# One chunk's rows turned by VectorE and DRAM loads instead of TensorE, the last tile's halves in PSUM banks of their own, its stores on two queues, and the order table written anew

## The chip, the cores and the metric

The kernel runs on one core of a Trainium2 chip. The metric is device time in microseconds of one launch, the median of several runs. Beside it stands one profiled execution, whose trace gives every row that is quoted here.

## What is computed

One transformer-like block over S = 2048 rows of D = 512 numbers, all in fp32, cut here to what matters:

```python
mod = (silu(c) @ w_mod)                       # six rows of 512: sa, ca, ga, sb, cb, gb
h = layernorm(x) * (1 + ca) + sa
q, k, v = split(h @ wqkv)                     # 32 heads of 16
phi(t) = concat(softmax(t @ w_phi), softmax(-(t @ w_phi)))
o = phi(q) (phi(k)^T v) / (phi(q) sum(phi(k)) + 1e-6)
x = x + ga * (o @ wo)
h = layernorm(x) * (1 + cb) + sb
x1 = h + shift(gelu(layernorm(h) @ w1)) @ w2  # quarters of the columns shifted by +1, -1, +2, -2 rows
x = x + gb * (x1 + gelu(layernorm(x1) @ w3) @ w4)
```

## The kernel before, in words

Rows are handled in 16 tiles of 128 and in 8 chunks of 256. Every exact product is made of three matmuls in a reduced format: each operand is split into a high and a low part (`hi_lo`, L480), and `three` (L471) issues high by high, high by low and low by high.

The work has three stages. The first goes over the chunks and forms k, v and q features and the running sums `kva` and `zacc` (groups named k, v, q, kv in the code). The second, `phase_a` (L950), goes over the chunks again: it finishes the attention (`num`), multiplies by `wo` (group o), normalises twice, and must then have the normalised rows turned, features on partitions, because the product with `w1` contracts over features. The third takes pairs of chunks through `w3` (`up`) and `w4` (`down_steps`) in products of seven instead of eight blocks, and `finish_rows` adds the residuals and stores the output.

In `phase_a` the turning is done by `to_T` (L902): four transposes of 128x128 on TensorE for each tile of 128 rows into a PSUM tile `pt`, then a high part by ScalarE or VectorE and a low part by VectorE. Elsewhere the kernel has another way: `normed` (L1152) writes rows whose columns are mixed in blocks of 32, lets VectorE turn the 32x32 blocks (`turn`, L686, tile `yt`), stores the tile to DRAM (`store_rows`), and loads it back with blocks exchanged by four DMAs (`load_turned`, L694). `turned_block` (L706) and `split_turned` (L716) are the same for a chunk; the list `BIAS["nturn"]` (L227) says which chunks of `phase_a` use them, and it is empty. Nothing else in the code decides it.

At the end of the third stage `down_steps` holds four PSUM tiles `ac` for a chunk. `acc[2]` and `acc[3]` belong to its two tiles of 128 rows, and each holds both halves of 256 columns in one bank. The remainder of F (96 rows of `w4`) is added by three matmuls of 512 columns per tile. In the very last chunk `finish_rows` adds and stores the halves one after the other; in the plan every PSUM tile counts as one piece, so the first half is not read before the last matmul into the other half is done. All stores and nearly all loads are issued from SyncE, whose queue works in order.

The order of all instructions is not found by the code but is written out: `ORDER` (L40) is a list of the numbers of some 2800 steps, with a letter where a step goes to another engine than its first choice (A, V, G), and `emit` runs through it. `SLOT` (L162) names the buffer of each tile. Each engine works through its own steps in this order, and waits where a step's operand is not there. In the trace a helper's line stands for its operations: L468 matmul, L477 transpose, L398 ScalarE, L415 VectorE, L417 GpSimd, L452 store.

Of the kernel before, what the change touches and what calls it, by code (L numbers as in the profile page):

```python
# [15 lines left out]
P = 128  # L16
# [144 lines left out]
)  # L161
SLOT = {  # L162
    "pp": "2112103775712644371760105367611260725752737061505556300230174572340654633645407076250504027663340302"
          "145552521507",
    "bd": "13",
    "w": "174625cd387165ad28cb09",
    "rk2": "5846",
    "x2": "9",
    "st": "1377h22bbb1155hh02hg88gbf79d90221",
    "mv": "0bh0e42j01f3f380d28hebh03dg0bc0bb",  # L170
# [193 lines left out]
def body(ctx: ExitStack, tc, x, wqk_t, wv_d, wo_d, w1_d, w2_d, w3_d, w4_d, c_d, wmod_d, id_d, cst_d, cst2_d, out):  # L364
# [7 lines left out]
    def T(tag, shape=(P, D), dt=FP):  # L372
        return plan.tile(shape, dt, tag)
# [1048 lines left out]
```

## Time and profile before

| | us |
|---|---|
| median of 3 runs (550.7 to 551.48) | 550.83 |
| the profiled execution's own time | 551.07 |
| its span, first to last instruction | 549.2 |
| TensorE busy | 541.0 |
| VectorE busy | 492.2 |
| GpSimd busy | 372.7 |
| ScalarE busy | 339.8 |

The profile's times are counted from the start of the span. Between the span and the profiled execution's own time lie 1.9 us, and that execution was 0.24 us above the median. A row of the timeline gives start, length, engine, line, operation, tiles and count, and in square brackets the idle time before it and what ended it.

### The profile page before, as it was taken

The page shows a single profiled execution, that of the slowest core. Times are in us where ns is not written, and L with a number is a line of the kernel's source. Part 1 is how long each engine was busy: PE and PEld are TensorE (multiplying, and loading weights), DVE is VectorE, ACT ScalarE, POOL GpSimd, SP SyncE. Part 2 cuts the span into 40 slices and gives each one's busy share as a digit, 9 for nine tenths or more (in the row PEclk, how much of TensorE's full clock was granted, in tenths as well). Part 3 has the DMA queues.
Part 4 walks back from the last instruction along what each step waited for, and adds up shares of the span by engine and source line. Part 5 has one row for each costly group of instructions (what it writes and reads, how often), then busy time and mean ns, then how long its engine had stood idle before and what let it go on. Part 6 is the DMA issues. An engine that isn't in the chain of part 4 may idle for free.

```text
span 549.2 us, 12264 instructions
## 1 busy us (share of the span) xinstructions
PE 541.0 (98%) x4474; PEld 484.0 (88%) x4474; DVE 492.2 (90%) x899; ACT 339.8 (62%) x800; POOL 372.7 (68%) x383
## 2 busy tenths in 40 slices
PE   7999999999999999999999999999999999999997
PEld 6888788888677887888889999999999999999996
DVE  4999999999999999999998988988889768988887
ACT  2799988734436896959898576873533535234430
POOL 2388988979599999998995264433655653355354
PEclk9999999999999999999999999999999999999999
DMA  8975364247485669886898899989469746592032
GB/s 320 350 242 211 109 186 157 77 140 235 135 225 183 194 205 296 253 271 233 234 309 315 274 351 328 361 329 326 192 184 389 245 174 237 191 356 87 1 117 76
DMA packets 63668, 124.89 MB, mean 227 GB/s; under 512 B 7060, under 2 KB 26772, under 8 KB 59512
## 3 DMA queue, kind: packets, MB, share of 16 engines
q1 hardware_dynamic: 63320, 124.04, 66.4%
q8 instruction: 35, 0.57, 0.5%
q14 instruction: 25, 0.20, 0.1%
q10 hardware_dynamic: 288, 0.07, 0.1%
HBM read 89.74 MB, written 34.35 MB: 226 GB/s over the span
## 4 chain that ended last, share of the span: by engine, by line
PE 84%; DVE 9%; DMA 2%; issue 2%; POOL 2%; ACT 1%; DVEq 0%; POOLq 0%
PE pp L468 32%; PE pa L468 28%; PE ac L468 20%; PE pt L477 3%; DVE q L439 2%; DMA mod<-in_wmod 1%; DVE k L439 1%; DVE pz L439 1%; DVE pT L688 1%; DVE ke L415 1%; DMA const<-in_c 1%; DVE qe L415 1%; POOL qe L417 1%; PE kva L468 1%; ACT n L398 0%
## 5 line engine op out<-in xcount | busy, mean ns | idle before, releaser
L468 PE MATMUL pp<-w,hh 128*128 128x512 f32 x576 | 138.2, 397 | 0.0
L468 PEld LDWEIGHTS pp<-w,hh 128*128 128x128 f32 x576 | 106.8, 188 | 25.3 <-issue 1.0
L468 PE MATMUL pa<-bH,wq 128*128 128x256 f32 x840 | 105.9, 281 | 0.0
L468 PE MATMUL ac<-w,gg 128*128 128x256 f32 x840 | 105.4, 281 | 0.0
L468 PEld LDWEIGHTS ac<-w,gg 128*128 128x128 f32 x840 | 102.9, 188 | 1.2
L468 PEld LDWEIGHTS pa<-bH,wq 128*128 128x128 f32 x840 | 102.7, 188 | 0.6
L417 POOL TENSOR_TENSOR gg<-cu,gg 128x128 fp32r<-128x128 f32 (+1 forms) x32 | 21.4, 675 | 40.7 <-PE ac L468 13.8
L468 PE MATMUL pp<-w,sh 128*128 128x512 f32 x192 | 47.9, 397 | 0.0
L468 PE MATMUL pp<-w,oT 128*128 128x512 f32 x192 | 47.1, 395 | 0.0
L468 PE MATMUL pa<-nT,w 128*128 128x256 f32 x384 | 46.2, 279 | 0.0
L468 PEld LDWEIGHTS pa<-nT,w 128*128 128x128 f32 x384 | 45.1, 188 | 0.9 <-ACT mv L592 0.2
L468 PEld LDWEIGHTS pp<-w,sh 128*128 128x128 f32 x192 | 35.1, 188 | 8.6 <-POOL sh L1050 0.5
L468 PEld LDWEIGHTS pp<-w,oT 128*128 128x128 f32 x192 | 35.6, 188 | 8.0
L585 POOL TENSOR_TENSOR rs<-mv,const 128x2 f32<-128x2 f32 x31 | 24.3, 785 | 24.5 <-ACT mv L592 22.9
L398 ACT ACTIVATE cu<-pa 128x512 f32<-128x512 f32 (+1 forms) x41 | 21.3, 525 | 31.0 <-PE pa L468 13.6
L398 ACT ACTIVATE gg<-cu 128x256 fp32r<-128x256 f32 (+1 forms) x48 | 16.5, 360 | 25.0 <-PE ac L468 22.4
L417 POOL TENSOR_TENSOR e<-e,q 128x1024 f32<-128x1024 f32 x15 | 29.9, 2009 | 0.0
L415 DVE TENSOR_TENSOR gg<-sg,gg 128x512 fp32r<-128x512 f32 x36 | 26.3, 736 | 4.0 <-ACT gg L398 2.7
L417 POOL TENSOR_TENSOR ez<-e,const 128x1024 f32<-128x1024 f32 x12 | 28.8, 2407 | 0.1
L417 POOL TENSOR_TENSOR ke<-ke,k 128x1024 f32<-128x1024 f32 x14 | 28.6, 2049 | 0.0
L398 ACT ACTIVATE gg<-sg 128x512 fp32r<-128x512 f32 x28 | 17.3, 625 | 18.1 <-DVE gg L407 6.7
L415 DVE TENSOR_TENSOR cu<-pa,cu 128x512 f32<-128x512 f32 (+1 forms) x36 | 21.0, 594 | 7.5 <-PE pa L468 5.9
(221 smaller groups left out, 1224.7 us busy)
## 6 DMA issues: line engine op xcount, KB each, us to landing
wq<-dram SPq DMA_DIRECT2D x32, 1024.0 KB, 7.3
dram<-ws SPq DMA_DIRECT2D x35, 256.0 KB, 3.9
dram<-qe SPq DMA_DIRECT2D x16, 512.0 KB, 3.5
e<-dram SPq DMA_DIRECT2D x64, 128.0 KB, 3.6
xl<-in_x SPq DMA_DIRECT2D x30, 256.0 KB, 3.9
raw<-in_w SPq DMA_DIRECT2D x18, 256.0 KB, 4.0
mod<-in_wmod SPq DMA_DIRECT2D x16, 256.0 KB, 4.9
dram<-xl SPq DMA_DIRECT2D x16, 256.0 KB, 3.8
```

The costliest lines, as they stand in the source:

```text
L398: nc.scalar.activation(o(), i(), func, **kw)
L415: dve = ("DVE", 71 + 1.04 * o.n + 90 * (isps(a) and isps(b)), lambda: nc.vector.tensor_tensor(o(), a(), b(), op=op))
L417: pool = ("Pool", cost, lambda: nc.gpsimd.tensor_tensor(o(), a(), b(), op=op))
L439: plan.op("DVE", 65 + 1.04 * a.n + 110 * isps(o), lambda: nc.vector.tensor_reduce(o(), a(), axis=AX.X, op=op), [o], [a])
L468: nc.tensor.matmul(o(), a(), b(), start=s, stop=e, **kw)
L477: nc.tensor.transpose(o(), i(), ident())
L585: plan.op("Pool", 540 + 10 * m, lambda: nc.gpsimd.tensor_tensor(r(), v(), mhalf[:, :m](), op=OP.pow), [r], [v, mhalf])
L688: plan.op("DVE", 71 + 1.04 * o.n, lambda: nc.vector.transpose(o(), i()), [o], [i])
```

## The change

It has four parts.

1. `BIAS["nturn"]` is `[7]`: the last chunk's rows in `phase_a` take the way over VectorE and DRAM. Eight transposes on TensorE go, with the two high and two low parts that read `pt`. Two turns on VectorE, two stores, four loads and two high and two low parts that read SBUF come.
2. In the last chunk the second tile's halves stand in PSUM banks of their own (`apart_` and `acc[3]`). The remainder's three matmuls of 512 columns for that tile become six of 256, and the second half is complete once its three are done.
3. The store of that tile's first half, which is now the last to be ready, is issued from ScalarE's queue; the second half's store stays on SyncE's.
4. `ORDER` and `SLOT` are written anew over the whole kernel. Beside the places below, some steps change engine: in the first stage some 15 steps leave VectorE and 13 come to it; in the third stage the steps that cut the activations to pieces move both ways.

```diff
-    "0 3 16 1 6 2 30 23 44 4 48 46 5 50 8 89 13 82 7 14 20 9 143 37 671 38 39 31 40 24 78G 41 142 32 15 33 12 27 25 "
+    "0 3 23 6 2 16 30 44 5 46 48 50 8 1 15 12G 27 9 14G 81 13G 10 7 11 80G 43G 24 31 79 4 32 37 89 82 38 39 33 143 "
...
-        6, 8, 9, 10, 11, 12, 13, 14, 15], "tw": "any", "zpe": [15], "nturn": [], "xturn": []}
+        6, 8, 9, 10, 11, 12, 13, 14, 15], "tw": "any", "zpe": [15], "nturn": [7], "xturn": []}
...
         acc = [T("ac", [P, 2, HD]) for _ in range(4)]
+        apart_ = T("ac", [P, HD]) if c == NC - 1 else None
...
                     sl = slice(t * P, (t + 1) * P)
+                    if t and apart_ is not None:
+                        for o, n, whole in ((apart_, slice(HD, D), True), (acc[3][:, 0, :], slice(HD), False)):
+                            mms(three(o, g[:n9, 0, sl], g[:n9, 1, sl], last["w4"][0][:n9, n], last["w4"][1][:n9, n], whole, whole),
+                                [o], [g, *last["w4"]], skip=True)
+                        continue
...
-                finish_rows(c, acc)
+                finish_rows(c, acc, apart_)
...
             for a in range(2):
-                tt(x1[:, a, :], x1[:, a, :], p[:, a, :], OP.add)
-                store(out[rows_, a * HD:(a + 1) * HD], x1[:, a, :], P * HD * 4)
+                tt(x1[:, a, :], x1[:, a, :], apart_ if t and a else p[:, a, :], OP.add)
+                if t and not a:
+                    plan.op("Activation", 60, lambda dst=out[rows_, :HD], i=x1[:, 0, :]: nc.scalar.dma_start(dst, i()), [], [x1[:, 0, :]],
+                            land=2400)
+                else:
+                    store(out[rows_, a * HD:(a + 1) * HD], x1[:, a, :], P * HD * 4)
```

The loop over `a` runs over 0 and 1; the new table puts the add of `apart_` ahead of the other.

The new table at three places. The first is TensorE's start. `mod` are the pieces of `w_mod`, `pt` the first chunk's turned rows. Before, one transpose group stands ahead of the last piece of `w_mod`:

```order
L468 MATMUL pp_183<-mod_11_91,const_180 32x256 x4
L477 MATMUL pt_202<-const_71,xn_188 128x128
L477 MATMUL pt_202<-const_71,xn_174 128x128
L477 MATMUL pt_202<-const_71,xn_188 128x128
L477 MATMUL pt_202<-const_71,xn_174 128x128
L468 MATMUL pp_183<-mod_14_100,const_180 32x256 x4
L477 MATMUL pt_214<-const_71,xn_188 128x128
```

Now, on the same engine:

```order
L469 MATMUL pp_180<-mod_11_91,const_118 32x256 x4
L469 MATMUL pp_180<-mod_12_93,const_118 32x256 x4
L478 MATMUL pt_207<-const_97,xn_178 128x128
L478 MATMUL pt_207<-const_97,xn_191 128x128
L478 MATMUL pt_207<-const_97,xn_178 128x128
L478 MATMUL pt_207<-const_97,xn_191 128x128
L478 MATMUL pp_214<-const_97,mod_212 128x128 x2
L478 MATMUL pt_217<-const_97,xn_178 128x128
```

All four pieces of `w_mod` now come first, and both transpose groups behind them; the set of steps ahead of the first projection is the same.

The second place is SyncE's queue where the last chunk of `phase_a` is turned. `h` are the rows that `w2` leaves, `raw` pieces of `w4`, `yt` turned rows, `zt` and `bL` the tiles loaded back. Before:

```order
L452 DMA dram_4170<-h_3282 128x512
L691 DMA dram_4176<-yt_4167 128x512
L445 DMA raw_4183<-in_w 128x512
L691 DMA dram_4176<-yt_4200 128x512
L452 DMA dram_4233<-h_3652 128x512
L445 DMA raw_4248<-in_w 128x512
L445 DMA xl_4251<-dram_4170 128x512
```

Now the chunk's own two stores (to dram_4179) and its four loads stand in that queue:

```order
L692 DMA dram_4179<-yt_4169 128x512
L692 DMA dram_4179<-yt_4173 128x512
L453 DMA dram_4192<-h_3291 128x512
L446 DMA raw_4195<-in_w 128x512
L446 DMA raw_4200<-in_w 128x512
L453 DMA dram_4218<-h_3633 128x512
L699 DMA zt_4237<-dram_4179 32x8x128 x4
L446 DMA xl_4263<-dram_4192 128x512
```

Two stores of `h` and two loads of `raw` stand between the stores of `yt` and the loads of `zt`, and the loads of the next pair of chunks (`xl`) behind them.

The third place is the end of TensorE's program. `ac_7447` is the last tile's accumulator, `gl` the remainder's activations. Before:

```order
L468 MATMUL ac_7447<-w_4598,gg_7320 128x256 x2
L468 MATMUL ac_7447<-w_4598,gg_7420 128x256
L468 MATMUL ac_7447<-w_1947,gl_7353 128x512 x3
L468 MATMUL ac_7447<-w_4650,gg_7363 128x256
L468 MATMUL ac_7447<-w_4695,gg_7363 128x256
L468 MATMUL ac_7447<-w_4650,gg_7437 128x256
```

Now `ac_7537` is the bank apart and `ac_7428` the other half's:

```order
L469 MATMUL ac_7537<-w_1986,gl_7366 128x256 x3
L469 MATMUL ac_7428<-w_4628,gg_7335 128x256 x2
L469 MATMUL ac_7428<-w_4628,gg_7364 128x256
L469 MATMUL ac_7428<-w_1986,gl_7366 128x256 x3
L469 MATMUL ac_7428<-w_4636,gg_7356 128x256
L469 MATMUL ac_7428<-w_4757,gg_7356 128x256
L469 MATMUL ac_7428<-w_4636,gg_7417 128x256
```

The second half is complete nine matmuls of 256 columns ahead of the end.

More of the change, by code (lines that the diff above doesn't have):

```diff
@@ L40 @@
 ORDER = (
[120 rows of a table removed]
[120 rows of a table added]
 )
 SLOT = {
-    "pp": "2112103775712644371760105367611260725752737061505556300230174572340654633645407076250504027663340302"
-          "145552521507",
-    "bd": "13",
+    "pp": "2017153341420272046716375311663140363222230515024276010257257623475043673604407762257504025763345262"
+          "267543421715",
+    "bd": "0i",
     "w": "174625cd387165ad28cb09",
[L167 to L170, printed above, removed]
@@ L171 @@
-    "rs": "29812hcbbjji851d0ie93863874jh6213",
-    "nm": "3fa4a54dde4e1jjcf2883583gaacj278gb331h60ed7ha0092e635b5a",
-    "xn": "10cg751eba368fe9",
-    "mod": "lh9g7ejf9i4638bkia",
-    "mod2": "0213",
+    "rk2": "1090",
+    "x2": "4",
+    "st": "200009ff736hb70d77884j2978da427f0",
+    "mv": "56672ff476h030h70ff4j26b9idb3hhaj",
+    "rs": "04b499hc30b4740d748hi7d90hb225200",
+    "nm": "31g3i74fg434h7c4h30b0aaa722dchicd26ab6gff226975d725fjff7",
+    "xn": "e0kg751e4i36b430",
+    "mod": "4a9g740f9i4638bkbi",
@@ L176 @@
+    "mod2": "2356",
     "kva": "4",
     "za": "7",
-    "hh": "30a89be0",
-    "pt": "06254521753213317025344576360400",
-    "raw": "da1k0d63f6hg40cljd4940abi353",
-    "k1": "2430035525435132",
+    "hh": "3da89be0",
+    "pt": "365135427532573005233464601705",
+    "raw": "daj1gd7l15dc780fjd4940abi353",
+    "k1": "1051002221432452",
     "ke": "4501639451823940",
-    "k2": "1213035252034134",
-    "vv": "ib4j953cdj19a75f",
-    "qe": "3792232883214942",
-    "q1": "2440243225135053",
-    "qt": "5e97g70fkccg",
@@ L188 @@
-    "xl": "abd42002jf51cl836e2i1h3b0j5g2je53k0hhej4hlahd0",
-    "acc": "cl8hi",
-    "kvs": "f",
-    "pz": "1",
-    "q2": "10141003",
-    "e": "5617956758034928",
-    "ez": "8348813999970750",
-    "q3": "2212223043334222",
-    "q5": "23253203",
-    "pT": "4272394975373487",
-    "oT": "99594b24",
-    "nT": "9999bb2e",
-    "n": "1931gfgfahafb63g",
+    "k2": "1215311215032431",
+    "vv": "98lf042l7k4k95i1",
+    "qe": "0792222881213942",
+    "q1": "3035311003431055",
+    "qt": "5e0ii8c5dc36",
@@ L201 @@
+    "xl": "l8d32h02jf518j041lb2gh3b01fg2je53k5hhej4hlafd0",
+    "acc": "cl8h6",
+    "kvs": "c",
+    "pz": "1",
+    "q2": "32131223",
+    "e": "5617946758034928",
+    "ez": "8338271399150770",
+    "q3": "0010002203000422",
+    "q5": "33200011",
+    "pT": "6852384627273007",
+    "oT": "9b44ee04",
+    "nT": "b9bb4b2e",
+    "n": "8b40f00iahajb63g",
     "h": "7kd9l62c7i1lfkcd",
-    "gf": "17555662",
-    "sh": "2520ecb0",
-    "pa": "762553462761040036271541705740316243253470661263027034160772",
+    "gf": "17537312",
@@ L205 @@
+    "sh": "e902ecb0",
+    "pa": "565753556037500036267547305740315243253470661263027054360772",
     "wr": "80061",
-    "ws": "khe217da8lk4eba05bb5dfgfd71i652ak90",
+    "ws": "khe21adb1ei66jai5e29gfjfd71e652ak9g",
+    "zt": "1",
+    "yt": "47e59k0dj7j90lb6aa",
     "gb": "8",
-    "tw": "98935",
+    "tw": "96935",
     "bL": "47604149",
-    "nb": "1ahb5c79egg4jc3f",
-    "yt": "e5jkbdh7j9l9a6cd",
-    "bH": "52804219431594595069127578657523",
-    "tr": "714eb039akdl4172",
+    "nb": "bfhbca79egg4jc3f",
@@ L214 @@
+    "bH": "52804210431994595069127578657523",
+    "tr": "21ga5j3e6hdlg17b",
     "wq": "490c934e174e3174e7314e7134ee3417e431",
-    "cu": "672egi14f3fl25b7c10g4hg9ked6l14g9cd0jblf",
-    "gl": "c3jca56i",
-    "ac": "26311567160267423016415376013542",
-    "gg": "32781952372584716531287609873295063284107962583012103241806937415809263740821596",
-    "sg": "bkbka76k6hk6h4kj6a25j37b2lbji26k2i2594k2",
+    "cu": "672egi14b3fl25b7c10g4hg9ked6l14g9cd0jblf",
+    "gl": "c3jca56f",
+    "ac": "263115671602674275104153760135423",
@@ L220 @@
+    "gg": "32781952872584716531287609863295063284157962583012103241806937415809263740821596",
+    "sg": "k0bka76k6hk46khj6a25j37b2lbjf2k65i2f94l2",
     "xb": "9had9ei0fc3ha71e",
-    "xc": "5lj03023672l0gfh",
-    "uu": "j3347ell",
+    "xc": "5lj00323442i0e96",
+    "uu": "2ik375gc",
 }
@@ L1334, in down_steps, with finish_rows @@
                 marks["down"] = done
-                finish_rows(c, acc)
+                finish_rows(c, acc, apart_)
             yield
-    def finish_rows(c, acc):
+    def finish_rows(c, acc, apart_):
         xs = []
```

238 rows, old and new, of the table ORDER are left out of this document.

## The prediction

> **What bounds the kernel now.** I read the page first: how long each engine is busy, and the chain of work that ended last by engine.
>
> ```profile
> span 549.2 us, 12264 instructions
> PE 541.0 (98%) x4474; PEld 484.0 (88%) x4474; DVE 492.2 (90%) x899; ACT 339.8 (62%) x800; POOL 372.7 (68%) x383
> PE 84%; DVE 9%; DMA 2%; issue 2%; POOL 2%; ACT 1%; DVEq 0%; POOLq 0%
> ```
>
> TensorE (PE) has work for 541.0 of 549.2 us. What it does not fill is 8.2 us, and no change of order can win more than a part of that; anything beyond must take work from PE. So the second view is PE's own waits.
>
> ```profile
> PE pp L468 <- DMA rk<-in_wqk_t: 1.8, 1, 1.8
> PE pp L468 <- DVE ke L415: 1.0, 1, 1.0
> PE pp L468 <- POOL const L495: 1.0, 1, 1.0
> PE pt L477 <- ACT n L398: 0.4, 1, 0.4
> ```
>
> There are four. Two (1.8 and 1.0) lie in the first 9 us; the other two, 1.0 and 0.4, are all that PE waits for between the start and the last matmul. The busy time by stage shows where these two come from.
>
> ```profile
> 125.00:145.00 20.00, 18.98 (x182) 14.35 (x181) 19.68 (x24) 7.75 (x16) 14.87 (x10) 1.00 0.62 204
> 165.00:184.00 19.00, 18.58 (x142) 14.60 (x141) 18.43 (x34) 13.99 (x32) 19.00 (x15) 1.00 0.56 191
> 290.00:330.00 40.00, 40.00 (x284) 37.34 (x284) 34.46 (x62) 29.46 (x78) 18.77 (x28) 1.00 0.91 314
> ```
>
> The columns are the stretch, its length, then busy us (and count) of PE, its weight loads, DVE, ACT, POOL, the granted clock, the DMA share and GB/s. From 125 to 184 us VectorE (DVE) is as full as PE, so PE and DVE bound that stretch together. Behind 184 us PE is full and DVE has room (34.46 of 40). Between 290 and 330 us, where the last chunk is turned, the DMA engines are busy 0.91 of the time.
>
> **The change part by part.** I work against the profiled execution, 551.07 us: the span of 549.2 and 1.9 us around it. The median of the runs, 550.83, is 0.24 lower, and I take that off at the end. A measurement of this kernel can tell about 0.2% from no change, 1.1 us.
>
> *The transposes.* The chain around chunk 7 holds both its groups:
>
> ```profile
> 305.25 2.86 PE pa L468 x24
> 308.11 0.44 PE pt L477 x4
> 308.55 1.42 PE pa L468 x12
> 309.97 2.77 PE pp L468 x12
> 312.74 0.44 PE pt L477 x4
> ```
>
> The chain gives start, length, what. Two groups of four at 0.44 are 0.88 us of PE that go, from a stretch where PE never waits: -0.88, if nothing takes their place. Another row gives the length of a single one:
>
> ```profile
> L477 PE MATMUL pt<-const,n x16: 270/273/273, 290.2 to 312.9; 128*128 128x128 f32 x16
> ```
>
> One lasts 273 ns, but four stand in 0.44 us, so a start follows the other after 110 ns, and that is what PE gets back. The Trainium skill, page "TensorE: Matmul & The Clock Gate", section "Part 4: PE-mode transpose", puts a 128x128 transpose at about 275 ns within a kernel. By that price eight would be worth an estimated 2.2 us and the change would come to about 548.2. The length of one in this trace agrees with the page; the price per transpose does not, because they overlap here, so I give that result no chance of its own.
>
> What comes instead runs elsewhere:
>
> ```profile
> L688 DVE STREAM_TRANSPOSE yt<-nb x16: 670/704/712, 261.0 to 371.3; 128x512 f32<-128x512 f32 x16
> DMA to landing us min/median/max: 2.0/3.7/6.3
> L698 SPq DMA_DIRECT2D bL<-dram x32: 318/448/1493, 267.0 to 467.1; - x32
> DMA to landing us min/median/max: 2.4/3.8/9.2
> L398 ACT ACTIVATE bH<-bL x14: 615/622/637, 276.9 to 499.2; 128x512 fp32r<-128x512 f32 x14
> ```
>
> These are the rows of the same way elsewhere in the kernel: the turn, its store's landing, the four loads, their landing, and the first part split off. Two turns cost DVE 1.4 us where it has 5.5 us free in 40. The high and low parts stay the same in number and size, so they cost nothing new. From the second turn's end to the first operand for `w1`: 0.3 to issue the store (as SyncE's other stores, quoted below), 3.7 to land, four loads at 0.45 to issue, 3.8 to land, 0.62 for the high part, about 0.7 for the low part: 10.9 us. What covers it is what the order table puts on PE between that turn and `w1` of chunk 7: eleven steps of three 512-wide matmuls (12 in 2.77, so 0.69 each, 7.6 us) and 60 of 256 columns (12 in 1.42, so 7.1 us): 14.7 us. With 3.8 us to spare I cost the way round at nothing. With the longest landings, 6.3 and 9.2, it is 18.9, and PE would wait 4.2 us: that is a rival below. Queued behind it on SyncE are the loads of the next pair of chunks, which PE needs only after `w1` of chunk 7; SyncE's four loads and two stores add 2.4 us of issue.
>
> *The split remainder.* Three matmuls of 512 columns (2.77/12 each, 0.69) become six of 256 (1.42/12 each, 0.71): +0.02, nothing. That these have 96 rows and not 128 bounds it no further than 0.1 either way.
>
> *The tail.* The end of the timeline:
>
> ```profile
> 543.97 1.29 POOL L417 TENSOR_TENSOR xb<-xb,uu 128x512 f32<-128x512 f32 x1 [0.26 <-DVE uu L415]
> 544.92 0.52 PE L468 MATMUL ac<-w,gg 128*128 128x256 f32 x3
> 545.54 0.75 DVE L415 TENSOR_TENSOR xb<-xb,ac 128x256 f32<-128x256 f32 x2 [0.99 <-PE ac L468]
> 545.99 0.33 SPq L452 DMA_DIRECT2D out_dram<-xb  x1
> 546.42 0.38 SPq L452 DMA_DIRECT2D out_dram<-xb  x1
> DMA to landing us min/median/max: 1.7/1.8/1.8
> ```
>
> The last three rows are the last two stores and their landing. From the chain come the first of the two adds alone, and the first DMA that ScalarE issues:
>
> ```profile
> 0.71 3.74 DMA const<-in_c
> ...
> 545.54 0.42 DVE xb L415
> ```
>
> PE ends at 545.44. Both halves are added after that (0.10 to start, 0.75 for both), the second store is issued 0.13 later and lands in 1.8: 548.2, 2.78 behind PE, and the span ends 1.0 later. Now the second half is complete nine matmuls earlier (9 x 0.118 = 1.06 us), its add of 0.42 and its store lie under those, and behind PE stand one add (0.10 + 0.42), an issue (0.03 to 0.13, by the first and the second store) and a landing. With 1.8 for the landing that is 2.40: -0.38. I take 1.8, since a store from the same tile to the same tensor is nearest. The only DMA from ScalarE that the chain shows took 3.74, and if that is its price the tail is 1.56 worse than with 1.8, not better. The add of the second half also waits for GpSimd's sum into that row, which before ended only 0.18 ahead of PE; in the new order its operand stands one VectorE step earlier, and if it is as late as before the last add slips by 0.15. The store's move to another queue wins almost nothing by itself: SyncE was free at 546.32, before the second store could go. The Trainium skill, page "DMA: Bandwidth & Descriptors", section "Issuing engines are not separate DMA queues", says that issuing from several engines saves only the issuing time; by it the move is worth no more than one issue, as these rows have it too, so a gain that is larger than my 0.38 could not come from the queue.
>
> *The start.* The pieces of `w_mod` and what PE does with them, in the timeline and in their own DMA rows:
>
> ```profile
> L445 SPq DMA_DIRECT2D mod<-in_wmod x4: 328/496/642, 2.7 to 4.8; - x4
> DMA to landing us min/median/max: 7.8/8.3/8.9
> 13.45 0.66 PE L477 MATMUL pt<-const,xn 128*128 128x128 f32 x4
> 14.04 0.64 PE L468 MATMUL pp<-mod,const 128*32 128x256 f32 x8
> 14.61 0.66 PE L477 MATMUL pt<-const,xn 128*128 128x128 f32 x4
> 15.50 3.74 PE L468 MATMUL pp<-bd,rk 128*128 128x128 f32 x32
> ```
>
> The last piece is issued at 4.8 and lands 8.9 later (the longest of the four), at 13.7; PE used that time for a transpose group and took the piece up at 14.04. Behind it stood 1.46 us up to 15.50. The loads ahead of the piece are the same now, so it lands at 13.7 again, and behind it stand this and a transpose group more (0.57): 13.7 + 1.46 + 0.57 = 15.73, +0.2 to +0.4. The second load of `in_wqk_t` is issued one place earlier, so the wait of 1.8 shrinks, but that time only goes into the wait for `w_mod`. The delay meets the stretch that DVE bounds: the wait of 1.0 for `ke` has the same PE work ahead of it in both orders and two DVE steps fewer, so PE comes later and DVE not, and the wait pays for the delay. Sum 0, with bounds from -1.0 (both middle waits go, +0.4 start) to +0.4.
>
> *The rest of the order.* Behind 184 us PE has no wait to lose, so the new order can only keep that or add. Its sets of steps ahead of `g0`, `u00` and the last chunks are the same; I take nothing, and bound it by 1 us, the size of the wait for `ke`, on the bad side.
>
> Sum: -0.88 + 0.02 - 0.38 = -1.24, so 549.8 for a profiled execution and 549.6 for the median.
>
> **The rivals.**
>
> *The order gives it back.* One wait of the size that stands at `ke` (1.0) appears behind 184 us, or the ScalarE landing is nearer to 3.74 than to 1.8. For it: 360 us without a wait is much to ask of a new order, and each step has only its own slack. Against it: DVE and ACT have room there. Time: 549.6 + 1.0 = 550.6, within 0.2% of before.
>
> *The middle waits go too.* DVE has two steps fewer ahead of `ke`, so 1.0 + 0.4 vanish and only the later start (0.4) is paid: another -1.0, 548.6. Against it: DVE is busy 19.68 of 20 there, and another step will be late next.
>
> *Slower: the way round over DRAM is late at `w1` of chunk 7.* The place is 290 to 330 us, where DMA is at 0.91 already; the chunk adds 1 MB, 3.3 us at 314 GB/s. It decides when the two landings together exceed 11.3 us (10.9 has 7.5 of landing, and 3.8 spare); the longest rows sum to 15.5. Then PE waits up to 4.2 us and the time is 549.6 + 4.2 = 553.8; a mean between costs 2.1, 551.7. Once PE stops, `u02` and all behind it in its program wait as well.
>
> That the transposes do not go, or that the halves still share a bank, I exclude: in the new order PE has no transpose of that chunk, and the half has a tile of its own.
>
> **How the numbers follow.** The sum as it stands 0.37, at 549.6. The middle waits going too 0.17 (548.6). Given back 0.32 (550.6). The late way round 0.14 (551.7 to 553.8). Faster by over 0.2% is below 549.73, so the forecast counts as faster by a narrow margin, and 0.01 of it I leave to no change: faster 0.36 + 0.17 = 0.53; within 0.2% 0.32 + 0.01 = 0.33; slower 0.14. The range runs from 548.2 (the case at 548.6, with 0.4 for a start that is not late) to 551.8, which takes in a tail 1.56 worse together with a wait of 0.6, and the mean of the late way round. Outside it lie the longer half of that rival and little else.
>
> **What would show it right or wrong.** Right: the groups of `pt` from `n` count 56 transposes in place of 64; PE's waits hold nothing new behind 184 us; the last add begins 0.1 behind the last matmul, is single, and its store from ScalarE's queue lands in about 1.8; the first projection begins 0.2 to 0.4 later, and the wait for `ke` is smaller by as much. Wrong: a wait of PE in `pa` for `nT` (the slower rival), any wait of 1 us behind 184 us (the first rival), a landing beyond 3 us at the end, or a wait for `ke` that is gone altogether with a sum below 549.

## The result, and the profile after

| | before | after |
|---|---|---|
| median of 11 runs each, us | 550.83 (550.62 to 551.60) | 554.75 (552.67 to 558.31) |
| ratio, 95% interval | | 1.0069 (1.0051 to 1.0087) |
| first profiled execution, span, us | 549.2 | 556.5 |
| second profiled execution, span, us | | 553.1 |

The change makes the kernel 0.7% slower, outside the range of the prediction. And it makes it unsteady: the runs of before lie within 1 us, those of after within 6. The first profiled execution after the change is the slowest of the eleven, so a second one was taken of the same kernel, and the accounts below rest on that one (554.9 us). With its eight runs the changed kernel has 19, and their median is 554.3.

The first page after the change, the same lines as before: length, busy time by engine, the chain that ended last.

```profile
span 556.5 us, 12263 instructions
PE 543.5 (98%) x4469; PEld 485.9 (87%) x4469; DVE 493.9 (89%) x891; ACT 343.5 (62%) x805; POOL 377.4 (68%) x388
PE 70%; POOL 8%; DMA 6%; DVE 5%; issue 3%; ACT 2%; SPq 1%; POOLq 0%; DVEq 0%
```

PE has fewer instructions and is busy for longer, and of the chain it holds 70% where it held 84%: GpSimd (POOL) and the DMA took what it lost. PE's waits in this first profile:

```profile
PE pp L469 <- POOL rs L568: 2.8, 1, 2.8
PE ac L469 <- POOL gg L418: 1.5, 2, 0.9
PE pp L469 <- POOL const L496: 1.0, 1, 1.0
PE pa L469 <- DVE h L416: 0.8, 1, 0.8
PE pp L469 <- DMA rk<-in_wqk_t: 0.7, 1, 0.7
PE pp L469 <- DVE hh L416: 0.6, 1, 0.6
PE pa L469 <- DMA wq<-dram: 0.4, 1, 0.4
PE pp L469 <- DVE bd L416: 0.4, 1, 0.4
PE pa L469 <- DVE h L435: 0.4, 1, 0.4
PE pt L478 <- ACT n L399: 0.3, 1, 0.3
PE ac L469 <- ACT cu L399: 0.3, 1, 0.3
PE ac L469 <- DVE cu L416: 0.2, 1, 0.2
```

Before, four rows were all; the wait for `ke` is gone, as one of the rivals had it, and others stand in its place. The second profile of the same kernel:

```profile
PE pp L469 <- POOL rs L568: 2.8, 1, 2.8
PE ac L469 <- POOL gg L418: 1.5, 2, 0.9
PE pp L469 <- POOL const L496: 1.0, 1, 1.0
PE pp L469 <- DVE bd L416: 0.5, 1, 0.5
PE pp L469 <- DVE hh L416: 0.4, 1, 0.4
PE pa L469 <- DVE h L435: 0.4, 1, 0.4
PE ac L469 <- ACT cu L399: 0.3, 1, 0.3
PE pt L478 <- ACT n L399: 0.3, 1, 0.3
PE pp L469 <- DMA mod<-in_wmod: 0.3, 1, 0.3
PE ac L469 <- DVE cu L416: 0.2, 1, 0.2
```

What stands in both lists belongs to the order (`rs`, `gg`, `h` of L435, `cu`); what stands in one alone (`wq`, `h` of L416, `rk`, `mod`) belongs to that run. The stretch from 290 to 330 us, read as before:

```profile
290.00:330.00 40.00, 40.00 (x293) 37.72 (x292) 33.63 (x65) 28.75 (x76) 18.27 (x29) 1.00 0.96 317
```

PE is full there after the change too: it does not wait at `w1` of the last chunk. The DMA share went from 0.91 to 0.96 (0.94 in the second profile).

The start, PE and then VectorE, in the first profile:

```profile
13.56 2.90 PE L469 MATMUL pp<-mod,const 128*32 128x256 f32 x32 [2.78 <-POOL rs L568]
...
21.82 0.95 PE L469 MATMUL pp<-w,hh 128*128 128x512 f32 x3
```

```profile
9.96 0.69 DVE L572 BATCH_NORM_STATS2 st<-x 128x6 f32<-128x512 f32 x1 [4.09 <-DMA x<-in_x]
```

`x` is now loaded behind the second piece of `in_wqk_t` and lands at 9.96, not 6.78; VectorE stands 4.09 us at its first use, and the steps that empty PE's banks (`w<-pp`, the first at 11.90) stand behind it in its queue. The first projection (`pp<-w,hh`) starts at 21.82, before at 18.99; in the second profile at 20.05.

**The granted clock.** The two profiles wait equally long for `rs` (2.78 and 2.81). In the first PE goes on 0.63 later than in the second, but its first projection is 1.77 later. What came between is TensorE's clock, in the stretch behind that wait (columns as before):

```profile
14.65:18.06 3.41, 3.37 (x24) 1.87 (x17) 1.72 (x5) 0.38 (x1) 0.00 (x1) 0.50 1.05 386
```

For 3.4 us the clock is 0.50, so PE can do up to 1.7 us less work in it. Eight of the profiles of this document hold such a stretch before PE's end, one of them (run 16) two. Each time PE had been busy for only 0.9 to 1.6 of the 3.4 us ahead of it. In the second profile PE is busy for 1.50 of such 3.4 us and the clock stays at 1.00, so the rule behind it is not shown. One such stretch takes 0.003 off a run's mean clock. None of the runs of the kernel before that stand beside the experiments has a mean below 0.998; of the 19 runs of the changed kernel five have 0.997 or less, with a median of 554.9 us, and the others 553.8. A wait thus costs more than its length in some runs, and part of the spread comes from there.

The end:

```profile
552.61 0.51 PE L469 MATMUL ac<-w,gg 128*128 128x256 f32 x3
553.16 0.42 DVE L416 TENSOR_TENSOR xb<-xb,ac 128x256 f32<-128x256 f32 x1 [0.56 <-PE ac L469]
553.66 0.35 ACTq L1376 DMA_DIRECT2D out_dram<-xb  x1
```

PE ends at 553.12, the last add is single, and the span ends 3.38 later, before 3.76: the tail gives 0.38. The transposes went:

```profile
L478 PE MATMUL pt<-const,n x56: 270/273/328, 185.2 to 293.1; 128*128 128x128 f32 x56
```

56 and not 64. One thing that no wait shows is the group of the `w1` product, in all 384 matmuls of the same form, before and in the second profile after (columns: busy us, mean ns, idle before):

```profile
L468 PE MATMUL pa<-nT,w 128*128 128x256 f32 x384 | 46.2, 279 | 0.0
```

```profile
L469 PE MATMUL pa<-nT,w 128*128 128x256 f32 x384 | 48.1, 282 | 0.4 <-DVE h L435 0.4
```

They take 1.9 us more for the same work.

**The account of the second profile**, 553.1 against 549.2 us. The first transpose group of `n` starts 0.27 later than before (183.74 against 183.47): the first projection was 1.06 late, and the middle repaid 0.79. The `w1` product is 1.9 longer. The waits behind 184 us that are new are `gg` 1.5, `h` 0.4, `cu` 0.3 and 0.2: 2.4. The transposes give 0.88, the tail 0.39 (3.37 behind PE). 0.27 + 1.9 + 2.4 - 0.88 - 0.39 = 3.3 of the 3.9; the rest lies in gaps too short for the list.

### The profile page after: what moved, and what is told of

Its sections match the earlier page's. It is cut to its first block, busy times and chain, and to the rows that moved or that the text cites. A ratio compares the mean times of both kernels' runs of the same rounds, so it can differ in the third digit from the quotient of the medians.

```text
span 556.5 us, 12263 instructions
## 1 busy us (share of the span) xinstructions
PE 543.5 (98%) x4469; PEld 485.9 (87%) x4469; DVE 493.9 (89%) x891; ACT 343.5 (62%) x805; POOL 377.4 (68%) x388
## 4 chain that ended last, share of the span: by engine, by line
PE 70%; POOL 8%; DMA 6%; DVE 5%; issue 3%; ACT 2%; SPq 1%; POOLq 0%; DVEq 0%
PE pp L469 29%; PE pa L469 21%; PE ac L469 17%; DMA dram<-yt 2%; DMA e<-dram 2%; POOL ez L418 2%; DMA wq<-dram 1%; PE pt L478 1%; POOL qe L418 1%; PE kva L469 1%; POOL gg L418 1%; POOL e L418 1%; DVE q L440 1%; DVE gg L416 1%; SPq L899 1%
## 5 line engine op out<-in xcount | busy, mean ns | idle before, releaser
L469 PE MATMUL pa<-nT,w 128*128 128x256 f32 x384 | 48.0, 282 | 0.4 <-DVE h L435 0.4
L469 PEld LDWEIGHTS pa<-nT,w 128*128 128x128 f32 x384 | 46.6, 188 | 1.9 <-DVE h L435 0.6
L418 POOL TENSOR_TENSOR gg<-cu,gg 128x128 fp32r<-128x128 f32 (+1 forms) x29 | 27.0, 937 | 18.4 <-DVE gg L408 7.1
L418 POOL TENSOR_TENSOR sg<-cu 128x128 f32<-128x128 f32 x25 | 12.9, 519 | 24.0 <-DVE gg L416 9.5
L416 DVE TENSOR_TENSOR gg<-sg,gg 128x512 fp32r<-128x512 f32 x35 | 24.8, 712 | 3.3 <-ACT gg L399 2.2
L399 ACT ACTIVATE ke<-ke 128x512 f32<-128x512 f32 x32 | 19.0, 624 | 13.7 <-DVE ke L416 13.6
```

Source lines behind the costliest of these rows:

```text
L399: nc.scalar.activation(o(), i(), func, **kw)
L416: dve = ("DVE", 71 + 1.04 * o.n + 90 * (isps(a) and isps(b)), lambda: nc.vector.tensor_tensor(o(), a(), b(), op=op))
L418: pool = ("Pool", cost, lambda: nc.gpsimd.tensor_tensor(o(), a(), b(), op=op))
L469: nc.tensor.matmul(o(), a(), b(), start=s, stop=e, **kw)
```

## The experiments

The theories, first two: A, the start (and with it the first stage) costs the time; B, new waits of TensorE in the third stage. Later came C, the way round holds up ScalarE and SyncE; D, the addresses in SBUF set the pitch of the `w1` product; E, the DMA traffic of the way round makes other loads late.

All ratios are against the kernel before on the same chip. Where a kernel is put together from the two order tables, a table is called OLD or NEW, and `NEW[:1760] + OLD` stands for the first 1760 steps of NEW and then all others in OLD's order.

**1. The changed kernel again.** No edit.

> The changed kernel unchanged, for a second profile of it (the first one, 558.31 us, lies 3.6 us above the median of 554.75). Theory A (the start: x arrives 3 us later, and the middle pays back about 1): first projection 2.8 us later than before, 1 to 2 of it left at the end. Theory B (new waits of TensorE behind 184 us): pieces that sum to 2 to 4 us there, in this profile as in the first. Median 554.7. If the extra waits behind 184 us are absent here, they belong to the first profile alone and the start must carry all of it.

553.15 us (552.48 to 557.74), ratio 1.0053 (1.0033 to 1.0073). The profile is the second one above. The waits behind 184 us for `gg` and `cu` are there again, so they belong to the order; those at 340 to 361 us are not.

**2. x ahead again.**

```diff
-0 3 23 6 2 16 30 44
+0 3 23 6 2 30 16 44
```

> The changed kernel with the load of x issued ahead of the second load of in_wqk_t again, nothing else moved. Theory A (the start is the cause): x lands 3 us earlier, VectorE's head of queue is free, first projection near 19.3 instead of 21.8, median 552.3 to 553 (2 to 2.5 better). Theory B (the later waits are the cause): first projection earlier too, but the gain is taken up by the middle waits, median 554 or above.

554.86 us, ratio 1.0072 (1.0058 to 1.0085): no gain, and theory A in this form falls. PE's start:

```profile
13.29 0.64 PE L472 MATMUL pp<-mod,const 128*32 128x256 f32 x8 [0.64 <-DMA mod<-in_wmod]
19.93 1.41 PE L472 MATMUL pp<-w,hh 128*128 128x512 f32 x5
```

With `x` in time PE waits for the pieces of `w_mod` instead, and all that follows them still stands behind: the first projection is 0.94 late without any lateness of `x`. So this run did not give the start of before back, and does not tell what a start in time would be worth.

**3. x late in the kernel before.**

```diff
-0 3 16 1 6 2 30 23 44
+0 3 16 1 6 2 23 30 44
```

> The kernel before with one swap: the load of x is issued behind both loads of in_wqk_t, as in the changed kernel. Theory A: VectorE stands 2 to 3 us at its first statistics, first projection 2 to 2.8 us later, median 552 to 553.2 (the middle waits take back up to 1). Rival (x has slack at the start, and the late projection of the changed kernel comes from the order of VectorE's steps): within 0.5 of 550.8.

553.26 us, ratio 1.0034 (1.0021 to 1.0047). The first projection starts at 21.15, 2.2 late, and PE ends 2.13 late. The wait for `ke` is as long as it was:

```profile
PE pp L470 <- DVE rs L428: 2.6, 1, 2.6
PE pp L470 <- DVE ke L417: 1.0, 1, 1.0
```

So the middle pays for a late PE only where VectorE is not late as well. `x` holds up VectorE first: its first statistics start at 8.20, before at 6.78. Behind the wait of 2.6 the clock is 0.50 from 11.85 to 15.26 us, so not all of the 2.2 is `x` alone: the three runs with the lower mean clock took 553.26 to 553.67, the other two 552.09 and 552.24.

**4. The tail alone.** The kernel before with the change's parts 2 and 3.

```diff
+                            mms(three(o, g[:n9, 0, sl], g[:n9, 1, sl], last["w4"][0][:n9, n], last["w4"][1][:n9, n], whole, whole),
...
+                    plan.op("Activation", 60, lambda dst=out[rows_, :HD], i=x1[:, 0, :]: nc.scalar.dma_start(dst, i()), [], [x1[:, 0, :]],
```

> The kernel before with only the tail's parts: the last tile's halves in banks of their own, the first half's store from ScalarE's queue; the order table as before but for the one step more, three matmuls of 256 columns. Prediction's step: 0.38 off, 550.45 by the median. Rival (the 0.38 seen in the changed kernel comes from its order): no change, 550.8.

550.52 us (550.37 to 551.29), ratio 0.9994 (0.9985 to 1.0002): 0.43 off by the medians, with an interval that just reaches no change. From PE's end to the span's end 3.44 us, before 3.76. It is the one part that can be taken as it is.

**5. The order without the way round.**

```diff
-"nturn": [7]
+"nturn": []
```

> The changed kernel's order without the way round over DRAM: the last chunk's rows are turned on TensorE as before, the tail's parts stay. Theory A (the order table costs the time, the parts are good): 0.9 more than the changed kernel, 554 to 555.6, and TensorE's waits near 397, 418 and 450 us stay. Theory C (the way round costs it: ScalarE and SyncE stand behind its loads and what follows comes late): the waits behind 340 us go, 550.5 to 552, and the runs spread less than the changed kernel's 552.5 to 558.

556.72 us by five of its six executions (556.17 to 562.19), ratio 1.0135 (1.0101 to 1.0169), slower than both theories. The sixth is the profiled one: it took 1367 us, with PE busy for 1359.8, and is not read. So this run tells nothing of the cause.

**6. and 7. The addresses.** The changed kernel with the places in SBUF that before gave its buffers, and the reverse. Nothing else is edited; only two large buffers, 5 and 9, have each other's place, since the larger of the two is not the same in both kernels.

```diff
+        if self.count == 1:
+            for j, w in enumerate(LAYOUT.split()):
+                tag, n = w.split(":")
+                pool.tile([P, int(n)], FP, tag=tag, bufs=1, name=f"lay_{j}")
```

> The changed kernel with the buffers of SBUF laid out as in the kernel before; the order and the buffer of each tile are the changed kernel's. In the changed kernel the 384 matmuls of the product with w1 (pa<-nT,w) are busy 48.1 us, before 46.2. Theory D (the addresses decide the pitch of these matmuls): back to 46.2, 1.5 to 1.9 us off the time. Rival (what runs beside them decides): 48.1 as it is, no change of time.

> The kernel before with the buffers of SBUF laid out as in the changed kernel, nothing else. Theory D: pa<-nT,w goes from 46.2 to about 48 us, and the time rises by as much, 552.3 to 552.7. Rival: 46.2 and 550.9.

The changed kernel came to 554.48 us (551.58 to 555.96), within its own spread; the kernel before to 551.55 (551.19 to 551.77), ratio 1.0010 (1.0001 to 1.0018). The group of the `w1` product, the changed kernel with the old addresses and then the old one with the new:

```profile
L483 PE MATMUL pa<-nT,w 128*128 128x256 f32 x384 | 47.3, 280 | 0.5 <-DVE h L449 0.4
```

```profile
L482 PE MATMUL pa<-nT,w 128*128 128x256 f32 x384 | 47.2, 282 | 0.0
```

Of the 1.9 us about half follows the addresses (0.8 one way, 1.0 the other), and the time of the steady kernel follows by 0.5. By chunk it is plainer: from start to start a matmul of this form takes 114.0 to 114.8 ns on average over a chunk wherever `nT` lies 181440 bytes behind the first buffer of the old list (`LAYOUT`), with its weights at 78848 and 164224, in the old order and in the new, 113.3 to 115.4 with `nT` at 173248, and 116.7 to 119.1 at all other places that these four kernels use. With the places of the new list all eight chunks of the old order take 117.6 to 118.1. The other half is then the choice of buffer for `nT`, which the new table changed as well, and buffer 9, which run 6 did not put back. Which bits of the address matter was not tried.

**8. Three steps from GpSimd to VectorE.**

```diff
-1935G ... 2037G ... 2055G
+1935 ... 2037 ... 2055
```

> The changed kernel with three low parts of the third stage (gg<-cu,gg 128x128) on VectorE in place of GpSimd, in the same place of the order. In the changed kernel TensorE waits 0.87 and 0.63 us for two of them, and GpSimd takes 2.28 us for one where 0.46 is usual. Theory B (new waits behind 184 us cost it): the two waits go, 1.5 us off, 551.7 to 553.3. Rival (VectorE is as late there, or the next step is): the waits stay in another name, 553 to 555.

552.79 us (550.72 to 557.73, 12 runs), ratio 1.0034 (1.0014 to 1.0055): 1.5 off the 554.3 of the 19 runs, and `gg` is gone from PE's waits. The waits are shown to go; the 1.5 is loose, since the unchanged kernel's own two sets of runs have medians 1.6 apart (554.75 and 553.15). GpSimd in the second profile of the changed kernel, around the first of the two waits:

```profile
393.56 0.46 POOL L418 TENSOR_TENSOR sg<-cu 128x128 f32<-128x128 f32 x1
395.62 2.28 POOL L418 TENSOR_TENSOR gg<-cu,gg 128x128 fp32r<-128x128 f32 x1 [1.60 <-DVE gg L408]
```

The same form takes 0.46 in the first row and 2.28 in the second, while VectorE works without a gap from 394.1 to 397.6; it ends 0.3 behind that run of steps, and PE takes up its next matmul at 397.96.

**9. Two steps to GpSimd in the kernel before.**

```diff
-1932 ... 2052
+1932G ... 2052G
```

> The kernel before with two low parts of the third stage (gg<-cu,gg 128x128) on GpSimd in place of VectorE, in their places of the order. Theory B's mechanism (a GpSimd step stands still while VectorE works through a run of steps on two SBUF operands): GpSimd takes over 2 us for at least one of them, and TensorE waits 0.5 to 1 for it near 395 us; 551.4 to 552.4. Rival (before has the slack, or GpSimd takes 0.46): 550.9.

550.76 us, ratio 0.9998 (0.9990 to 1.0007): the rival. Two low parts of this size behind 395 us take 0.45 and 0.46; the first of them:

```profile
396.72 0.45 POOL L417 TENSOR_TENSOR gg<-cu,gg 128x128 fp32r<-128x128 f32 x1
```

So the move to GpSimd costs nothing by itself in this order. That it costs where it falls into a full stretch of VectorE's work fits both runs, but is not tried apart. A long step alone costs nothing either: one of the same form takes 1.65 at 353.6 in the kernel before, and PE waits for none.

**10. The third stage old.** `NEW[:1760] + OLD`.

```diff
-ORDER = NEW
+ORDER = NEW[:1760] + OLD
```

> The changed kernel with the order of its third stage as in the kernel before: the table is the changed kernel's up to the last chunk's w2 (about 345 us), from there what is left stands in the order of before; all parts of the change stay. Theory B (new waits in the third stage): TensorE's waits near 397, 418 and 450 us go, 2.6 us off the changed kernel's 554.3 (median of its 19 runs), 551.2 to 552.2. Theory A (the start and the first stage): no more than 0.5 off.

552.81 us (550.73 to 556.70), ratio 1.0039 (1.0020 to 1.0058): 1.5 off where 2.6 was expected, and as loose as in run 8. The waits for `gg` and `cu` are gone, but its profile (554.4) has one of 1.8 for `wq` at 355.5 that the second profile of the changed kernel had not, and behind it the clock is 0.50 from 358.7 to 362.1 us. The floor fell from 552.5 to 550.7, the spread stayed.

**11. and 12. The first stage old, and all old but the last chunk's part.**

```diff
-ORDER = NEW
+ORDER = OLD[:870] + NEW
```

```diff
-ORDER = NEW
+ORDER = OLD[:870] + NEW[:1760] + OLD
```

> The changed kernel with the order of the start and the first stage as in the kernel before (up to the first chunk's product with w1, about 188 us), from there the changed kernel's. Theory A: first projection back at 19.0, and the runs lie as close together as those of before (within 1 us), since VectorE and GpSimd meet there in another order; 552.5 to 553.5. Theory B: the waits near 397, 418 and 450 stay and hold at least 2.5 us of the loss, so not under 552.5 either; if the time is below 552, B is wrong.

> The first stage and the third in the order of before, the new order only from the first product with w1 to the last chunk's w2 (188 to 345 us), with the way round over DRAM and the tail's parts. If the parts are worth what the prediction said and the order alone cost the time: 0.88 and 0.38 off, 549.6, with up to 0.5 more for the wait for h near 191 us. If the way round itself costs (theory C): 551 or more.

561.29 us (ratio 1.0187, 1.0173 to 1.0201) and 553.79 (1.0065, 1.0053 to 1.0078): the first worse than every theory, the second inside theory C's "551 or more". Both have waits near the seam that neither kernel has (1.2 and 1.0 for `oT` at 177 and 179 us): eight and six buffers had to go where neither table had them. So neither is counted for or against a theory, and most of the 10 us of the first is not accounted for.

**13. The way round in the old order.** The seam at another place, every buffer where one of the tables had it.

```diff
-ORDER = NEW
+ORDER = OLD[:1480] + NEW[:1690] + OLD
```

> The order of the kernel before up to the last chunk's second normalisation (about 300 us) and again from its w2 (about 340 us), the changed kernel's order only between; the way round over DRAM and the tail's parts are in. Differs from the run with the old first and third stage in that the seam lies at 300 us and every buffer has the place that one of the two kernels gave it. If the parts hold what the prediction said: 549.6 and runs within 1 us. Theory E (the 1 MB more on DMA engines that are 0.88 to 1.00 busy from 290 to 360 us makes the loads of wq late at 345 to 361 us): a wait of TensorE for wq or h of 0.5 to 2.8 there, in some of the runs, 550 to 552.5, and a spread over 1.5.

551.50 us (550.50 to 556.98, 12 runs), ratio 1.0025 (1.0006 to 1.0044): inside theory E's range and not the 549.6 of the sum, and the spread of 6 us comes with the way round into an order that was steady. The `w1` product is at 46.1 there. Its profile is of one of the faster runs (551.21) and has no wait for `wq` or `h`, so what the slow ones wait for is not seen.

**14. Its traffic alone.** The kernel of 4, with two stores and four loads that nobody waits for.

```diff
+    yd, z = T("dram", [TPC * P, D]), T("apart", [P, 7, NK, 32])
+    for t, y in enumerate(beside):
+        store_rows(yd, t, y)
...
+    plan.op("SP", 4 * 475, load_beside, [z], [yd], land=4500)
```

> The kernel before with the tail's parts and its last chunk still turned on TensorE, and beside that the DMA traffic of the way round alone: the chunk's two stores to DRAM and the four loads (seven eighths of their bytes) at the places that they have in the changed kernel, into a buffer that nobody reads. Without the traffic this kernel took 550.52. Theory E: landings of wq rise from 7.3 to 9 us or more, TensorE waits at 345 to 361 us in some runs, median 0.3 to 2 higher, spread wider. Rival (the loads have the slack): 550.5 and within 1 us as without.

554.20 us (551.60 to 555.11, 7 runs), ratio 1.0047 (1.0030 to 1.0065), against 550.52 without the traffic: 3.7 by the medians, with no work of any engine added but issues and DMA. That is more than the 2 that theory E allowed. SyncE's queue in the timeline, without the traffic and with it:

```profile
314.09 0.40 SPq L448 DMA_DIRECT2D wq<-dram  x1
315.63 0.38 SPq L448 DMA_DIRECT2D wq<-dram  x1
```

```profile
313.08 1.80 SPq L1406 DMA_DIRECT2D apart<-dram  x4
315.94 1.89 SPq L449 DMA_DIRECT2D wq<-dram  x1
319.87 0.72 SPq L449 DMA_DIRECT2D wq<-dram  x1
```

The DMA issues from 300 to 333 us (KB each, median us to landing), without and with:

```profile
wq<-dram SPq DMA_DIRECT2D x5, 1024.0 KB, 8.1
```

```profile
wq<-dram SPq DMA_DIRECT2D x5, 1024.0 KB, 10.1
```

And PE with the traffic:

```profile
329.98 1.44 PE L472 MATMUL pa<-bH,wq 128*128 128x256 f32 x5 [2.75 <-DMA wq<-dram]
```

The second of these loads of 1 MB is issued at 319.87 in place of 315.63, since it stands in SyncE's queue behind the four loads, which stand behind the landing of the two stores: 1.85 of the 4.24 are there ahead of the first of them, 1.5 are its own longer issue (1.89 for 0.40), the rest is a longer stop ahead of the load between. The five of its kind land in 10.1 us at the median, without the traffic in 8.1. 4.2 later and 2 longer ate what slack there was and 2.75 more. The wait stands at 330 us and not at 345 to 361, where theory E had it.

The clock adds to it:

```profile
329.51:332.92 3.41, 2.94 (x13) 2.95 (x14) 0.00 (x0) 2.98 (x6) 2.66 (x3) 0.50 1.04 396
```

The twelve matmuls behind the wait take 2.93 us, without the traffic 1.60. By the mean clock four of the seven runs hold such a stretch (554.20 to 555.11) and three do not (551.60 to 552.62). So the traffic costs 1.1 to 2.1 us without it, and the 3.7 is the wait and the clock together.

**15. The first stage new.** The kernel of 4 with the new table's first 870 steps.

```diff
-ORDER = OLD
+ORDER = NEW[:870] + OLD
```

> The kernel before with the tail's parts, its last chunk turned on TensorE, and only the start and the first stage (up to 188 us) in the changed kernel's order. Theory A' (the changed first stage is faster when VectorE and GpSimd don't meet, up to 1 us, and up to 2 slower when they do or when x is late): median 549.5 to 552 against 550.52, and runs spread over 2 us or more. Theory E (the spread comes from DMA at 345 to 361): runs within 1 us.

553.89 us (551.68 to 556.27), ratio 1.0051 (1.0033 to 1.0068): 3.4 slower than without, spread 4.6. In its profile the start is 1.9 late and repaid by 184 us; three waits for `n` (1.2 in all) and one for `h` (0.4) between 184 and 279 us and a `w1` product of 47.3 in place of 46.2 make up most of the loss. One of the three waits (0.4) stands in run 4 as well, and five buffers, among them one of `n` and one of `h`, have a place that neither table gave them, so the waits are not surely the changed kernel's. The first stage itself ends nearly in time (183.61 us, in run 4 183.16); the loss is seen behind it. The spread stands here without the way round: five of the eight runs have the lower mean clock (553.63 to 556.27; in the profile it is 0.50 from 13.3 to 16.7 us), three not (551.68 to 553.56). A second source of spread shows in two profiles of the same code, run 1 and run 8, which differ only behind 390 us. VectorE, each:

```profile
66.97 2.55 DVE L416 TENSOR_TENSOR ws<-wr 128x256 f32<-128x256 f32 x1
```

```profile
66.95 0.63 DVE L416 TENSOR_TENSOR ws<-wr 128x256 f32<-128x256 f32 x1
```

One step, begun at the same time to 0.02 us, takes 0.63 or 2.55. What runs on GpSimd beside it, in run 1 and then, its second step, in run 8:

```profile
66.60 0.74 POOL L418 TENSOR_TENSOR ws<-ws 128x256 fp32r<-128x256 f32 x1
67.29 1.95 POOL L418 TENSOR_TENSOR ke<-ke,k 128x1024 f32<-128x1024 f32 x1
```

```profile
67.25 2.13 POOL L418 TENSOR_TENSOR ke<-ke,k 128x1024 f32<-128x1024 f32 x1
```

GpSimd has the same two steps in both runs, in run 8 each 0.04 earlier. In run 1 VectorE's step is the long one; in run 8 it is short, and GpSimd's second step takes 0.18 more. In run 1 VectorE's step ends 0.28 behind GpSimd's, and VectorE is 1.9 us behind from there on; at 184 us PE is 1.24 apart in the two runs.

**16. The order without the way round, once more.** As 5, with the last chunk's neighbourhood in the old order.

```diff
-ORDER = NEW
+ORDER = NEW[:1480] + OLD[:1650] + NEW
```

> The changed kernel's order and tail without the way round over DRAM, the last chunk's neighbourhood (about 300 to 335 us) in the order of before: a cleaner form of the second-batch run without the way round, in which the seam made TensorE wait. Theory E (late loads are a cost of the way round in the changed kernel too): its waits at 345 to 361 us gone, the 0.88 of the transposes back, 552.5 to 554.5 against the changed kernel's 554.3; the third stage's waits near 397, 418 and 450 stay. Order alone: 555.2, the 0.88 more and nothing less.

556.27 us, ratio 1.0105 (1.0079 to 1.0132). There is a wait of 2.6 for `sh` from GpSimd at 303.6 us, again one that neither kernel has. Whether the way round costs the changed order anything on the whole stays open: there PE waits 1.2 (`h` and `wq`) between 340 and 361 us in the first profile and not at all in the second.

## Why the prediction was wrong

The sum stands for a span of 548.0 us (549.2 less 1.24); the second profile has 553.1. By the account above the two gains came as forecast, and of the 5.1 between, 2.4 are waits behind 184 us, 1.9 the pitch of the `w1` product, 0.3 the start, and the rest short gaps.

*The transposes: right.* 56 remain, PE does not wait at `w1` of the last chunk, and the rival that put the wait there did not happen. The price of 110 ns each was not contradicted by any run.

*The tail: right.* 0.38 was forecast, 0.38 and 0.39 measured in the changed kernel, 0.32 between PE's end and the span's end where the tail was changed alone. The bad case beside it was reckoned wrongly: a landing of 3.74 makes the tail 1.94 worse than one of 1.8 and 1.56 worse than the kernel before. The range adds the 1.56 to 549.6, which has the gain in it already, so its upper end is 0.4 low; the measured time lies beyond either end. From the issue of the last store to the end of the span it is 2.84 us from ScalarE's queue, 2.78 before from SyncE's.

*The way round: the sum looked at the wrong wait.* "I cost the way round at nothing" held for the one consumer that the step followed. What stands behind it in SyncE's queue was named, and put aside with "which PE needs only after `w1` of chunk 7; SyncE's four loads and two stores add 2.4 us of issue". The traffic alone, in the old order, moved such a load by 4.2 and lengthened it by 2, and cost 3.7 us with the clock (run 14); a queue that works in order waits there for the stores to land as well as for the issues. The slower rival had the right place and named the full DMA engines, and had the wrong victim. In the changed kernel itself this cost is seen in one profile only: the first waits 0.8 for `h` and 0.4 for `wq` between 340 and 361 us, the second not at all.

*The start: "+0.2 to +0.4", "The loads ahead of the piece are the same".* They are not in the same order: `x` went behind a piece of `in_wqk_t`. The first projection is 1.06 late in one profile and 2.83 in the other, where the clock was 0.50 for 3.4 us. That the delay is paid by the wait for `ke` ("PE comes later and DVE not") is right where only PE is late (0.79 of 1.06 repaid), and wrong where `x` holds up VectorE too (run 3: 2.13 of 2.2 stays). Undoing the place of `x` won nothing (run 2), but left the projection 0.94 late. In the second profile 0.27 of the start is left at 184 us, inside the bound of 0.4. The new first stage put into the old order costs 3.4 (run 15), a part of it by clock, by addresses and by buffers that moved; how much of that the changed kernel pays is open.

*"The rest of the order: I take nothing, and bound it by 1 us".* This is the step that failed most. In the account above the waits behind 184 us are 2.4, where nothing was taken and 1 was the bound. With the old order of the third stage (run 10), or three steps back on VectorE (run 8), the waits for `gg` go and the medians are 1.5 lower. Its argument was that DVE and ACT have room there; room over 40 us says nothing of the few microseconds in which a step must be done. It also took a wait at its length; by the clock it can cost more.

*No step at all for the matmuls' own pitch.* 384 matmuls of unchanged form got 1.9 us longer. About half of it is shown to follow the places of their operands (runs 6 and 7), and the pitch by chunk ties the rest to the other buffers that `nT` got. This was in no term and no bound.

That GpSimd's steps stand still while VectorE works on two SBUF operands, and the other way round, is argued from the rows of runs 1, 8 and 9, not tried by itself. The Trainium skill, page "SBUF — State Buffer", section "Who interferes with whom", says that a VectorE instruction with two SBUF inputs contends with a GpSimd instruction that reads SBUF, that the ports they share are an exclusive lock, and that issue order decides who blocks. The lengths agree: 2.28 for 0.46 on GpSimd, ending 0.3 behind VectorE's run, and 2.55 for 0.63 on VectorE, ending 0.28 behind GpSimd's step. The order is not so plain: VectorE's long step starts 0.32 ahead of the GpSimd step that it outlasts, and behind another one. By that rule the new table is not one time but several, by who comes first.

The parts were measured one at a time at 1.5 (third stage), 3.4 (first stage) and 3.7 (traffic), more than the whole change lost, so they cannot simply be added; that a later PE waits less for a late load would explain it, but is not shown. How they share the loss in the changed kernel is not settled beyond the account of one profile. The fastest kernel of all is the one before with the tail alone, 550.52.

## What to carry to other kernels

A new order is a change of every queue, not only of the places that the change is about: list for each queue what was moved past what (loads, first of all), and ask of everything behind a moved DMA how much slack it had, its landing included. An engine's free share over tens of microseconds is no cover for a step on GpSimd that falls into a full stretch of VectorE. Look at the spread of the runs as well as the median, and at the granted clock behind each wait of about 2 us: here such a wait could cost up to 1.7 us (half of a stretch of 3.4) beyond its length in some runs and nothing more in others.

## What the runs showed of the hardware

In four kernels a matmul of one form (128x128 weights, 256 columns) repeats every 113.3 to 115.4 ns or every 116.7 to 119.1 ns by the SBUF addresses of its operands, with the clock at 1.00 in both. A VectorE step of 0.63 us took 2.55 in another run of the same code, with the start equal to 0.02 us. About 0.9 MB more (two stores of 256 KB and four loads of 112) in a stage whose DMA engines were 0.95 busy went with landings of the 1 MB loads of 10.1 us in place of 8.1 in run 14; in run 13, with the way round itself, they stayed at 7.7. And TensorE's granted clock fell to 0.50 for 3.4 us in eight of the profiles, behind 3.4 us in which PE had been busy for 0.9 to 1.6.
